# Transposing the second half of x with VectorE and transfers instead of TensorE

## The chip, the cores and the metric

The kernel runs on one core of a Trainium2 chip. The core has five engines with queues of their own: TensorE (matrix products into PSUM), VectorE, ScalarE, GpSimd (called POOL in the profile) and SyncE (SP, which here only issues transfers). The metric is the device time of one execution in microseconds. Times of runs are compared by their median; the profile covers one execution.

## What is computed

Two branches on the same x (2048 tokens, 448 features) are mixed by a gate for each token. Branch A is a diagonal state space layer with complex states, branch B a two-layer network with 1792 hidden units. All inputs are bf16.

```python
x = A_x                                   # [1, 2048, 448]
g = sigmoid((x * gate_w).sum(-1, keepdims=True))
# A: Lam_bar = exp(dt * Lam), B_bar = ((Lam_bar - 1) / Lam)[:, None] * Bmat
Bu = einsum("bld,pd->blp", x, B_bar)
for t in range(L):
    h = Lam_bar * h + Bu[:, t, :]
a = 2.0 * einsum("blp,dp->bld", hseq, Cmat).real + x * Dskip    # hseq: all h
b = silu(x @ w1) @ w2
return g * a + (1 - g) * b
```

## The kernel before

**Tiles and stages.** The tokens are cut into four stretches of 512 (`NCH = 4`, `CH = 512`), numbered 0 to 3. x is loaded with tokens on the partitions (`xnat`), four blocks of 128 tokens to a stretch. The products with w1 and with B contract over the features, so they need x with features on the partitions: `xT`. The 448 features are covered by four column groups of 128 that start at `XCOL = [0, 128, 256, 320]`; the last two overlap.

For each stretch: transposes of x (`x0_transposes` for stretch 0, `x_transposes` at line 498 for the others), products with w1 (tiles F) and B (tiles B) in `x_products` (matmul at line 663), evictions of the products from PSUM in `evict` (line 623): F tiles by ScalarE with silu into `aT` (line 634), B tiles into `U`, whose seven slots hold the states' inputs; for stretch 0 VectorE copies them (line 640), for the others ScalarE (line 642). Then `lanes` (line 706) on VectorE turns U by a rotation (COS, SIN), runs seven scans along the tokens (line 736) that write `Gf`, and turns the result back into `H`, one tensor for each stretch. For stretches 0 to 2 the scan's result comes back as bf16 (into U) by transfers that POOL issues (line 390). `ffn2` (line 768, matmul at 774) is the second layer of B, evicted by ScalarE (line 780) and added to the rest by an accumulating transfer of POOL (line 782). `readout` (line 786, matmul at 795) is the product of H with C, combined by VectorE (line 798) and stored by SP (line 801). `gates` (line 833) makes the gate and multiplies `xnat` in place by Dskip.

A transpose of stretches 1 to 3 is 32 TensorE transposes of 64 x 64 blocks into two PSUM banks (line 508), and two copies of 1024 elements into `xT`, by ScalarE (line 518) or, for one half of stretch 1, by VectorE (line 516).

**Order.** TensorE's order is the program's: the calls in the last lines of the kernel (864 to 883). All other engines are ordered by a list planner (`Plan.order`, line 104) when the kernel is built. It gives each operation a start by an estimated cost; among the operations of an engine that could start earliest it takes the one with the lowest priority number. In the calls `DVE(fn, reads, writes, cost, prio)` and `P.add(engine, ...)` the last numbers are these. `lanes(tc)` has priority 20 + tc, `gates` 19, parameters 3 to 3.5, U evictions 2.6 on VectorE and 5 on ScalarE. An issue of a load costs 0.5 us on SP, its data are put at 300 GB/s in one pipe, with 0.9 us ahead and 0.8 behind. On the chip each engine keeps the planned order and waits with semaphores (`Waits.put`) for what an operation reads or overwrites, however late that is.

Names that the change touches: `H[3]` is the state of stretch 3 and, early in the run, holds B's rows (`Bnat`) as they were loaded; after their transposes it lies unused until `lanes(3)`. `xn2`, `xn3` are the names of the loads of stretches 2 and 3; SP issues them last of all loads.

Of the kernel before, what the change touches and what calls it, by code (L numbers as in the profile page):

```python
# [11 lines left out]
BF16 = DT.bfloat16  # L12
I32 = DT.int32

S_TOK = 2048
D_MOD = 448
F_FF = 1792
CH = 512
# [4 lines left out]
NOT = 5  # L23
NWARM = 6
NFILL = 2
XCOL = [0, 128, 256, 320]

TURN = 6.283184
# [248 lines left out]
def bass_gated_mix__ssm_conv_s5__dense_activation_silu__prompt_kernel(nc, A_x, A_Lambda_re, A_Lambda_im, A_B_re, A_B_im, A_C_re, A_C_im,  # L277
               A_log_dt, A_Dskip, B_x, B_w1, B_w2, gate_w, out):
    with ExitStack() as ctx:
# [6 lines left out]
        x2, out2 = A_x[0], out[0]  # L286

        xnat = sb("xnat", [128, NTB, D_MOD], BF16)
        xT = sb("xT", [128, 4, S_TOK], BF16)
        w1s = sb("w1s", [128, 4, F_FF], BF16)  # L290
        w2s = sb("w2s", [128, NFB, D_MOD], BF16)
        BT = sb("BT", [128, 4, 896], BF16)
# [175 lines left out]
        def x0_transposes(q0, part, who):  # L468

            tk = Ps(2)  # L470

            def mm(pe):
                for q in (q0, q0 + 1):
                    for k in range(2):
                        o = ((q - q0) * 2 + k) * 64
                        for h in range(2):
                            p = slice(64 * h, 64 * h + 64)
                            r = pe.transpose(bk(tk, h).bitcast(BF16)[:, o:o + 64], xnat[p, 2 * part + k, XCOL[q]:XCOL[q] + 128], ident[p, p])  # L478
                return r
            PE(mm, [f"xn0{part}", "ident"], [tk], 4 * 0.054, "xT0")  # L480
            for h in range(2):
                src = lambda h=h: bk(tk, h).bitcast(BF16)[:, 0:256].rearrange("p (q b n) -> p q b n", q=2, n=64)
                dst = xT[:, q0:q0 + 2, 256 * part:256 * part + 256].rearrange("p q (b h n) -> p q b h n", h=2, n=64)[:, :, :, h, :]
                names = [f"xT0_{q}{part}{h}" for q in (q0, q0 + 1)]
                if who[h] == "d":
                    DVE(lambda e, src=src, dst=dst: e.tensor_copy(dst, src()), [tk], names, 0.28, 0, "xTe")  # L486
                else:
                    ACT(lambda e, src=src, dst=dst: e.activation(dst, src(), AF.Copy), [tk], names, act_cost(256), 0, "xTe")
# [4 lines left out]
        x0_transposes(2, 1, "dd")  # L493

        xn_of = {tc: {q: [f"xT{tc}_{h}" for h in range(2)] for q in range(4)} for tc in range(1, NCH)}
        xn_of[0] = {q: [f"xT0_{q}{part}{h}" for part in range(2) for h in range(2)] for q in range(4)}

        def x_transposes(tc, who):

            tk = Ps(2)  # L500

            def mm(pe):
                for q in range(4):
                    for b in range(4):
                        o = (q * 4 + b) * 64
                        for h in range(2):
                            p = slice(64 * h, 64 * h + 64)
                            r = pe.transpose(bk(tk, h).bitcast(BF16)[:, o:o + 64],  # L508
                                             xnat[p, 4 * tc + b, XCOL[q]:XCOL[q] + 128], ident[p, p])
                return r  # L510
            PE(mm, [f"xn{tc}", "ident"], [tk], 16 * 0.035, f"xT{tc}")
            for h in range(2):
                src = lambda h=h: bk(tk, h).bitcast(BF16).rearrange("p (q b n) -> p q b n", q=4, b=4)
                dst = xT[:, :, tc * CH:(tc + 1) * CH].rearrange("p q (b h n) -> p q b h n", h=2, n=64)[:, :, :, h, :]
                if who[h] == "d":
                    DVE(lambda e, src=src, dst=dst: e.tensor_copy(dst, src()), [tk], [f"xT{tc}_{h}"], 0.69, 2.2, "xTe")
                else:
                    ACT(lambda e, src=src, dst=dst: e.activation(dst, src(), AF.Copy), [tk], [f"xT{tc}_{h}"], act_cost(1024), 2.2, "xTe")

        cosn = [f"COS{k}" for k in range(4)] + ["COSd"]  # L520
        sinn = [f"SIN{k}" for k in range(4)] + ["SINd"]
# [101 lines left out]
        def evict(pair, tk):  # L623

            kinds = [t[0] for t in pair]
            for k, n in ((0, 2),) if pair[0][:2] == pair[-1][:2] and len(pair) == 2 else ((0, 1), (1, 1))[:len(pair)]:
                kind, tc, a = pair[k]
                step = pair[k + 1][2] - a if n == 2 else 1
                sl = slice(a, a + step * (n - 1) + 1, step)
                names = [t[2] for t in pair[k:k + n]]  # L630
                src = (lambda: bk2(tk)) if n == 2 else (lambda k=k: bk(tk, k)[:, None, :])
                if kind == "F":
                    dst = aT[tc % 2][:, sl, :]
                    ACT(lambda e, src=src, dst=dst: e.activation(dst, src(), AF.Silu),  # L634
                        [tk, "tbl"], [f"aT{tc % 2}_{m}" for m in names], act_cost(512 * n), 2.5, "silu")
                    continue
                U, un = UG[tc % 2], f"U{tc % 2}_"
                dst = U[:, sl, :]
                if tc == 0:
                    DVE(lambda e, src=src, dst=dst: e.tensor_copy(dst, src()), [tk], [f"{un}{m}" for m in names], 0.15 + 0.53 * n, 2.6, "U")  # L640
                else:
                    ACT(lambda e, src=src, dst=dst: e.activation(dst, src(), AF.Copy), [tk], [f"{un}{m}" for m in names], act_cost(512 * n), 5, "U")  # L642
                if 3 in names:
                    load("pool", U[0:64, 7, :], U[64:128, 3, :], un + "7a", 65536, 9, [un + "3"])
                    load("pool", U[64:128, 7, :], U[0:64, 3, :], un + "7b", 65536, 9, [un + "3"])

        def x_products(tiles, fill={}, wait=()):

            part = (list(zip([(i, 64) for i in (0, 1, 2, 3)], [(i, 0) for i in (0, 1, 3, 2)])),
                    list(zip([(i, 0) for i in (0, 1, 2)], [(i, 64) for i in (0, 1, 3)])))
            pairs = [tiles[t:t + 2] for t in range(0, len(tiles), 2)]
            toks = [Ps(2) for _ in pairs]

            def steps(k, h, a, z):
                def body(pe):
                    for n, cut in list(enumerate(part[h]))[a:z]:  # L660
                        for b, ((i, p0), tile) in enumerate(zip(cut, pairs[k])):
                            tc = tile[1]
                            r = pe.matmul(bk(toks[k], b), weights(tile, p0, p0 + 64, i), xT[p0:p0 + 64, i, tc * CH:(tc + 1) * CH],  # L663
                                          start=(h == 0 and n == 0), stop=(h == 1 and n == 2))
                    return r
                reads = [n for cut in part[h][a:z] for (i, _), tile in zip(cut, pairs[k])
                         for n in xn_of[tile[1]][i] + (w1n(tile[2], i) if tile[0] == "F" else btn[tile[2]])]
                return PE(body, list(dict.fromkeys(reads)), [toks[k]], (z - a) * PE_MM[512], f"{pairs[k][0][0]}{pairs[k][0][1]}")

            def half(k, h):  # L670
                if h == 0 and pairs[k][0] == ("F", 0, 0):
                    def zero(pe):
                        for n in range(NFILL):
                            for b, p in enumerate((slice(64, 128), slice(0, 64))):
                                r = pe.matmul(bk(toks[k], b)[:, 0:128], ones[p, 0:128], ones[p, 0:128], start=True, stop=True)  # L675
                        return r
                    PE(zero, [], [toks[k]], NFILL * 0.11, "fill")
                    steps(k, 0, 0, 2)
                    steps(k, 0, 2, 4)
                else:  # L680
                    steps(k, h, 0, len(part[h])).own = h == 1
                if h:
                    evict(pairs[k], toks[k])

            half(0, 0)
            for f in fill.get(-1, ()):
                f()
            for k in range(len(pairs)):
                order = [lambda: half(k, 1)] + [lambda: half(k + 1, 0)] * (k + 1 < len(pairs))
                for n, f in enumerate(order if k - 1 in wait else order[::-1]):  # L690
                    f()
                    for m in fill.get((k, n), ()):
                        m()
                for f in fill.get(k, ()):
                    f()
# [173 lines left out]
        gates(0)  # L869
        gates(1)  # L870
        lanes(1)
        for f in cp(0) + G(0, 1) + cp(1, 2) + G(2, 3) + cp(3):
            f()
        x_products(F(1) + F(2, 0, 1) + B(2), {2: xt(2, "aa")})
        gates(2)
        lanes(2)
        for f in G(4, 5, 6, 7) + C(0, 1, 2, 3):
            f()
        x_products(F(2, 1) + B(3) + F(3), {1: xt(3, "aa"), 9: [lambda: gates(3), lambda: lanes(3)]})
        for f in C(4, 5, 6, 7) + G(8, 9, 10, 11):  # L880
            f()
        for f in C(8, 9, 10, 11) + G(12, 13, 14, 15) + C(12, 13, 14, 15):
# [36 lines left out]
```

## Time and profile before

| what | us |
|---|---|
| runs: median of three (lowest, highest) | 141.94 (141.46, 142.53) |
| the profiled execution | 141.25 |
| its span | 139.5 |
| TensorE busy | 135.9 |
| VectorE busy | 122.0 |
| ScalarE busy | 90.3 |
| POOL busy | 39.2 |
| L663, products with xT, share of the chain | 46% |
| L774, second layer of B, share of the chain | 31% |
| L795, readout, share of the chain | 15% |
| L508, transposes of stretches 1 to 3, share of the chain | 1% |
| SP, last issue of a load; first store | 21.8; 70.3 |

The span runs from the first to the last instruction in the profile; 1.75 us of the execution lie around it. All times inside the profile count from the span's start. Engine names with q (SPq) are the queue's own work: issues of transfers. The chain of work that ended last is followed back from the last instruction to whatever released it. "Idle before" an instruction is in brackets with what ended it. In the profile UG is the tensor that holds U.

### The profile page before, as it was taken

The numbers are of one execution on the slowest core, as the hardware profiler recorded it, in microseconds if no ns is written. First come the engines' busy times: TensorE is split into PE (matmuls) and PEld (weight loads), VectorE is DVE, ScalarE is ACT, GpSimd is POOL, SyncE is SP. The second block draws the span as 40 slices with busy tenths as digits, with TensorE's granted clock in tenths as the row PEclk, the third lists the DMA queues.
The fourth block names the chain that finished last, engine by engine and source line by source line (L and its number), as shares of the span: only waits on it lengthen the run. The fifth ranks groups of instructions, "written<-read, shape, count | busy, mean of one in ns | idle before, by whom it ended". The sixth has DMA issues, their size and how long they took to land.

```text
span 139.5 us, 3000 instructions
## 1 busy us (share of the span) xinstructions
PE 135.9 (97%) x1201; PEld 67.0 (48%) x1201; DVE 122.0 (87%) x179; ACT 90.3 (65%) x157; POOL 39.2 (28%) x72
## 2 busy tenths in 40 slices
PE   7999999999999999999999999999999999999992
PEld 2445454455544544455544544444455555555561
DVE  0319999999999999999999999999999999997053
ACT  3349768999989999823694887799931268312300
POOL 7134040100248440227733001824000314022220
PEclk9999999999999999999999999999999999999999
DMA  4998999510156770104976200674202322323242
GB/s 136 337 294 243 363 320 238 177 42 0 31 79 94 129 110 1 38 15 73 157 131 155 38 5 0 95 133 79 38 4 97 66 33 36 83 83 61 40 94 71
DMA packets 17956, 14.71 MB, mean 105 GB/s; under 512 B 2835, under 2 KB 17814, under 8 KB 17942
## 3 DMA queue, kind: packets, MB, share of 16 engines
q0 software_dynamic: 6064, 5.51, 24.8%
q1 hardware_dynamic: 11318, 8.65, 20.7%
q10 hardware_dynamic: 560, 0.36, 0.8%
q8 instruction: 9, 0.15, 0.4%
q14 instruction: 5, 0.04, 0.1%
HBM read 7.17 MB, written 1.84 MB: 65 GB/s over the span
## 4 chain that ended last, share of the span: by engine, by line
PE 97%; DVE 0%; issue 0%
PE ps L663 46%; PE ps L774 31%; PE ps L795 15%; PE ps L463 2%; PE ps L508 1%; PE ps L478 1%; PE ps L814 1%; PE ps L604 1%; DVE ot L798 0%; PE ps L675 0%; PE ps L464 0%; PE ps L536 0%
## 5 line engine op out<-in xcount | busy, mean ns | idle before, releaser
L663 PE MATMUL ps<-xT,w1s 64*128 64x512 bf16 x392 | 48.5, 378 | 0.0
L774 PE MATMUL ps<-w2s,aT 128*128 128x448 bf16 x224 | 43.2, 353 | 0.0
L634 ACT ACTIVATE aT<-ps 128x1024 bf16<-128x1024 f32 (+1 forms) x30 | 28.7, 969 | 8.5 <-PE ps L663 8.4
L774 PEld LDWEIGHTS ps<-w2s,aT 128*128 128x128 bf16 x224 | 21.7, 98 | 20.4 <-ACT xnat L849 0.4
L663 PEld LDWEIGHTS ps<-xT,w1s 64*128 64x128 bf16 x392 | 19.7, 94 | 22.3 <-DVE xT L486 0.7
L663 PE MATMUL ps<-xT,BT 64*128 64x512 bf16 x196 | 25.8, 376 | 0.0
L782 POOL DMA_DIRECT2D xnat<-fe x16 | 14.1, 900 | 37.9 <-ACT fe L780 37.2
L780 ACT ACTIVATE fe<-ps,g 128x448 bf16<-128x448 f32 x16 | 10.1, 632 | 21.1 <-PE ps L774 21.0
L390 POOL DMA_DIRECT2D UG<-Gf x27 | 14.7, 549 | 20.9 <-DVE Gf L736 20.4
L736 DVE TENSOR_TENSOR_SCAN Gf<-rc,gin,H 128x512 f32<-128x512 f32 x14 | 17.2, 1268 | 0.0
L795 PE MATMUL ps<-CP,H 128*128 128x448 bf16 (+2 forms) x98 | 16.4, 326 | 0.0
L663 PEld LDWEIGHTS ps<-xT,BT 64*128 64x128 bf16 x196 | 10.8, 94 | 11.1 <-DVE Gf L562 0.2
L798 DVE SCALAR_TENSOR_TENSOR ot<-ps,g,xnat 128x448 bf16<-128x448 f32 (+2 forms) x18 | 10.8, 622 | 6.0 <-issue 4.6
L390 POOL DMA_DIRECT2D UG<-UG x8 | 4.8, 597 | 29.2 <-ACT UG L642 17.4
L704 DVE TENSOR_TENSOR H<-UG,COS 128x3584 bf16<-128x3584 bf16 (+4 forms) x10 | 12.6, 1266 | 0.0
L795 PEld LDWEIGHTS ps<-CP,H 128*128 128x128 bf16 x98 | 8.9, 98 | 7.5 <-DVE k L752 0.4
L642 ACT ACTIVATE UG<-ps 128x1024 bf16<-128x1024 f32 (+1 forms) x12 | 10.7, 923 | 1.4 <-PE ps L663 1.4
L842 ACT ACTIVATE junk<-xg 128x448 bf16<-128x448 bf16 x16 | 9.2, 574 | 2.1 <-DVE xg L704 2.0
L849 ACT ACTIVATE xnat<-xnat,g 128x448 bf16<-128x448 bf16 x16 | 9.8, 671 | 0.2
L704 DVE TENSOR_TENSOR PI<-UG,SIN 128x512 bf16<-128x512 bf16 (+2 forms) x13 | 9.1, 722 | 0.0
L704 DVE TENSOR_TENSOR PO<-UG,SIN 128x1536 bf16<-128x1536 bf16 (+1 forms) x8 | 8.7, 1087 | 0.1
L736 DVE TENSOR_TENSOR_SCAN Gf<-rc,gin,H2C 128x512 f32<-128x512 f32 x7 | 8.5, 1265 | 0.0
(102 smaller groups left out, 126.5 us busy)
## 6 DMA issues: line engine op xcount, KB each, us to landing
UG<-Gf POOLq DMA_DIRECT2D x21, 128.0 KB, 2.5
xnat<-fe POOLq DMA_DIRECT2D x16, 112.0 KB, 2.6
out_dram<-ot SPq DMA_DIRECT2D x15, 112.0 KB, 1.7
w2s<-in_B_w_dram SPq DMA_DIRECT2D x1, 1568.0 KB, 11.8
xnat<-in_A_x_dram SPq DMA_DIRECT2D x3, 448.0 KB, 6.1
w1s<-in_B_w_dram SPq DMA_DIRECT2D x1, 576.0 KB, 6.2
UG<-UG POOLq DMA_DIRECT2D x8, 64.0 KB, 2.2
H2C<-in_A_C_re_dram SPq DMA_DIRECT2D x2, 196.0 KB
```

Of the source, the lines that this page charges most:

```text
L390: P.add(q, lambda e: e.dma_start(dst, src), list(after), name.split(), 0.6 if q == "pool" else 0.5, prio, sem(), nbytes, tag="ld " + name)
L634: ACT(lambda e, src=src, dst=dst: e.activation(dst, src(), AF.Silu), [tk, "tbl"], [f"aT{tc % 2}_{m}" for m in names], act_cost(512 * n), 2 ...
L642: ACT(lambda e, src=src, dst=dst: e.activation(dst, src(), AF.Copy), [tk], [f"{un}{m}" for m in names], act_cost(512 * n), 5, "U")
L663: r = pe.matmul(bk(toks[k], b), weights(tile, p0, p0 + 64, i), xT[p0:p0 + 64, i, tc * CH:(tc + 1) * CH], start=(h == 0 and n == 0), stop=( ...
L704: DVE(lambda e: e.tensor_tensor(o, a, b, op), r, w, dve_cost(n, 2), prio, tag)
L736: DVE(lambda e, s=s, b=b, init=init: e.tensor_tensor_scan(Gf[:, s, :], rc[:, b:b + 1].to_broadcast([128, CH]), A[:, s, :], init, ALU.mult, ...
L774: r = pe.matmul(bk(tk)[:, 0:D_MOD], aT[tc % 2][:, fb, o:o + 128], w2s[:, fb, :], start=(fb == 0), stop=(fb == NFB - 1))
L780: ACT(lambda e: e.activation(f[:, :], bk(tk)[:, 0:D_MOD], AF.Copy, scale=g1[:, tb:tb + 1]), [tk, f"g1_{tc}"], [fn], act_cost(448, 1), 7, "fe")
L782: P.add("pool", lambda e: e.dma_start(Tb[:, tb, :], f[:, :], accum_op=ALU.add), [fn, f"Tb{tb}"], [f"Tb{tb}"], 0.94, 2, sem(), 115000, tag= ...
L795: r = pe.matmul(bk(tk)[:, 0:b - a], H[tc][:, s, o:o + 128], CP[:, s, a:b], start=(s == 0), stop=(s == NSLOT - 1))
L798: DVE(lambda e, tk=tk, a=a, b=b: e.scalar_tensor_tensor(ot[tb % NOT][:, a:b], bk(tk)[:, 0:b - a], g[:, tb:tb + 1], Tb[:, tb, a:b], ALU.mul ...
L849: ACT(lambda e, tb=tb: e.activation(Tb[:, tb, :], xnat[:, tb, :], AF.Copy, scale=g[:, tb:tb + 1]), [f"xd{tc}", f"g_{tc}"], [f"Tb{tb}"], ac ...
```

## The change

x of stretches 2 and 3 is no longer transposed by TensorE. `x_blocks(tc)` has VectorE transpose `xnat` in blocks of 32 by 32 into a scratch that lies in `H[3]`, with four instructions (two token blocks at a time, first the three column groups from 0, then the one from 320). In such a transpose each group of 32 partitions stays in place, so what is still to be done is to carry blocks from one partition group to another: 16 transfers (4 source groups g, 4 target groups m), each from 32 partitions to 32 partitions, 512 runs of 64 bytes, 32 KB, issued by SP with priority 400. Both stretches use the same scratch, so the transposes of stretch 3 wait for the transfers of stretch 2. The transposes have priority 15 for stretch 2 and 20.5 for stretch 3.

`xT` is laid out with the stretch first and the column group second. Of the seven U slots of stretch 0, evicted as (0, 1), (2, 3), (4, 5) and (6), the last three go to ScalarE.

```diff
+XPRIO = {2: 15, 3: 20.5}
+XBLK = (2, 3)
+UDVE = (0, 2)
...
-        xT = sb("xT", [128, 4, S_TOK], BF16)
+        xT = sb("xT", [128, NCH, 4, CH], BF16)
...
+        for tc in XBLK:
+            xn_of[tc] = {q: [f"xT{tc}_{g}{m}" for g in range(4) for m in range(4)] for q in range(4)}
...
+        def x_blocks(tc):
+
+
+            X32 = H[3][:, 0:4, :].rearrange("p m (q b i) -> p m q b i", q=4, i=32)
+            names = [f"H3_{s}" for s in range(7)] + ["H3_3i"]
+            xs = xnat[:, 4 * tc:4 * tc + 4, :]
+            for q0, q1, c in ((0, 3, 0), (3, 4, XCOL[3])):
+                n = q1 - q0
+                for b0, b1 in ((0, 2), (2, 4)):
+                    src = xs[:, b0:b1, c:c + 128 * n].rearrange("p b (q m i) -> p b q m i", q=n, i=32)
+                    dst = X32.rearrange("p m q b i -> p b q m i")[:, b0:b1, q0:q1, :, :]
+                    DVE(lambda e, dst=dst, src=src: e.transpose(dst, src), [f"xn{tc}"], names, 0.15 + 256 * n / 960, XPRIO[tc], "xTd")
+            k = sem()
+            for g in range(4):
+                for m in range(4):
+                    to = xT[32 * m:32 * m + 32, tc, :, :].rearrange("p q (b g i) -> p (q b) g i", b=4, i=32)[:, :, g, :]
+                    P.add("sp", lambda e, to=to, g=g, m=m: e.dma_start(to, X32[32 * g:32 * g + 32, m, :, :, :].rearrange("p q b i -> p (q b) i")),
+                          names, [f"xT{tc}_{g}{m}"], 0.5, 400, k, 32768, tag="xTm")
...
-                if tc == 0:
+                if tc == 0 and a in UDVE:
                     DVE(lambda e, src=src, dst=dst: e.tensor_copy(dst, src()), [tk], [f"{un}{m}" for m in names], 0.15 + 0.53 * n, 2.6, "U")
                 else:
                     ACT(lambda e, src=src, dst=dst: e.activation(dst, src(), AF.Copy), [tk], [f"{un}{m}" for m in names], act_cost(512 * n), 5, "U")
...
-                            r = pe.matmul(bk(toks[k], b), weights(tile, p0, p0 + 64, i), xT[p0:p0 + 64, i, tc * CH:(tc + 1) * CH],
+                            r = pe.matmul(bk(toks[k], b), weights(tile, p0, p0 + 64, i), xT[p0:p0 + 64, tc, i, :],
...
         lanes(1)
+        if 2 in XBLK:
+            x_blocks(2)
         for f in cp(0) + G(0, 1) + cp(1, 2) + G(2, 3) + cp(3):
             f()
-        x_products(F(1) + F(2, 0, 1) + B(2), {2: xt(2, "aa")})
+        if 3 in XBLK:
+            x_blocks(3)
+        x_products(F(1) + F(2, 0, 1) + B(2), {2: xt(2, "aa")} if 2 not in XBLK else {})
...
-        x_products(F(2, 1) + B(3) + F(3), {1: xt(3, "aa"), 9: [lambda: gates(3), lambda: lanes(3)]})
+        x_products(F(2, 1) + B(3) + F(3), {1: xt(3, "aa") if 3 not in XBLK else [], 9: [lambda: gates(3), lambda: lanes(3)]})
```

More of the change, by code (lines that the diff above doesn't have):

```diff
@@ L482, in x0_transposes @@
                 src = lambda h=h: bk(tk, h).bitcast(BF16)[:, 0:256].rearrange("p (q b n) -> p q b n", q=2, n=64)
-                dst = xT[:, q0:q0 + 2, 256 * part:256 * part + 256].rearrange("p q (b h n) -> p q b h n", h=2, n=64)[:, :, :, h, :]
+                dst = xT[:, 0, q0:q0 + 2, 256 * part:256 * part + 256].rearrange("p q (b h n) -> p q b h n", h=2, n=64)[:, :, :, h, :]
                 names = [f"xT0_{q}{part}{h}" for q in (q0, q0 + 1)]
@@ L513, in x_transposes @@
                 src = lambda h=h: bk(tk, h).bitcast(BF16).rearrange("p (q b n) -> p q b n", q=4, b=4)
-                dst = xT[:, :, tc * CH:(tc + 1) * CH].rearrange("p q (b h n) -> p q b h n", h=2, n=64)[:, :, :, h, :]
+                dst = xT[:, tc, :, :].rearrange("p q (b h n) -> p q b h n", h=2, n=64)[:, :, :, h, :]
                 if who[h] == "d":
```

## The prediction

> **What bounds the kernel now.** I began with the page's busy shares and the chain that ended last, in order of time. Columns of the chain: start, length, what ran.
>
> ```profile
> PE 135.9 (97%) x1201; PEld 67.0 (48%) x1201; DVE 122.0 (87%) x179; ACT 90.3 (65%) x157; POOL 39.2 (28%) x72
> ```
>
> ```profile
> 45.55 0.47 PE ps L508 x32
> ...
> 77.23 0.47 PE ps L508 x32
> ...
> 131.38 5.35 PE ps L795 x42
> 136.73 0.02 issue
> 136.75 0.35 DVE ot L798
> ```
>
> TensorE is the chain from 0.76 to 136.73 us with no gap. The two L508 entries, the TensorE transposes of x's third and fourth stretch, are what the change takes out of it.
>
> Then the timeline of VectorE, because the change adds work there:
>
> ```profile
> 18.43 1.22 DVE L640 CAST UG<-ps 128x1024 bf16<-128x1024 f32 x1
> 19.57 0.42 DVE L524 TENSOR_SCALAR Gf<-Gf 128x512 f32<-128x512 f32 x1
> 19.90 0.68 DVE L640 CAST UG<-ps 128x512 bf16<-128x512 f32 x1
> 20.50 0.68 DVE L516 COPY xT<-ps 128x1024 bf16<-128x1024 bf16 x1
> ...
> 42.73 5.67 DVE L736 TENSOR_TENSOR_SCAN Gf<-rc,H 128x512 f32<-128x512 f32 x5
> 48.32 2.00 DVE L704 TENSOR_TENSOR H<-UG,COS 128x3584 bf16<-128x3584 bf16 x1
> ...
> 126.07 2.09 DVE L704 TENSOR_TENSOR H<-H,PO 128x2048 bf16<-128x2048 bf16 x2
> 132.80 0.69 DVE L798 SCALAR_TENSOR_TENSOR ot<-ps,g,xnat 128x448 bf16<-128x448 f32 x1 [4.64 <-issue]
> ```
>
> VectorE has practically no idle time from 14 us until 128.16 (126.07 + 2.09), when it finishes H3, the state of the last stretch. TensorE reads H3 first at 131.38. So VectorE has a slack of 3.22 us, about 3.1 after the 0.1 that the planner counts for the signal, and everything added to its queue after 14 us, work or waiting, comes off this slack one for one. TensorE is the bound with a second bound 3 us behind it.
>
> Last the DMA view, cut to two windows: 15.9 to 18.6 us (rows of 896 B) and 22.0 to 22.5 (mostly the 128 B rows of C).
>
> ```profile
> DMA packets 1153, 1.03 MB, mean 381 GB/s; under 512 B 6, under 2 KB 1153, under 8 KB 1153
> q1 hardware_dynamic: 1153, 1.03, 109.0%
> ```
>
> ```profile
> DMA packets 228, 0.09 MB, mean 186 GB/s; under 512 B 151, under 2 KB 224, under 8 KB 228
> q1 hardware_dynamic: 216, 0.08, 84.5%
> ```
>
> Shares are of 16 engines. An 896 B packet held an engine 1.09 x 16 x 2.7 / 1153 = 40.8 ns. In the second window 0.845 x 16 x 0.5 = 6.76 us; less 65 large ones (2.65) leaves 151 small ones 27 ns each. The same sum gives 13 ns in 21.6 to 22.0 and 48 ns in 22.5 to 23.0. A small packet is not much cheaper than a large one.
>
> **The change part by part.** *TensorE* loses 2 x 0.47 = 0.94 us. That is all the change can gain: everything else in the chain stays. The new layout of xT costs nothing: the moving operand is 512 contiguous elements before and after (L663, 376 to 378 ns); nothing covers it, so a slower read would go straight into the span.
>
> *ScalarE* takes over one eviction of two slots and one of a single slot: 1.03 + 0.60 us by its own L642 rows, about 1.4 as starts follow ends 0.1 early. It loses four L518 copies, 1.95 at 46.51 and 1.93 at 78.19. Its idle pieces between 16 and 22 us (0.91, 0.84, 0.40, 0.47) hide the addition. Without that cover the banks of U come free up to 1.4 us late and TensorE waits for a bank; 0.94 of it would be paid by the transposes that fall away.
>
> *VectorE* loses the 18.43 and 19.90 casts: start to start 1.14 + 0.60 = 1.74 us. It gains eight transposes, per stretch two of 768 elements per partition and two of 256, together 2048. No row shows a transpose. Bounds: the quickest form, the SBUF copy of 1536 bf16 in 0.53, is 0.25 ns an element with the 0.146 fixed that L704 shows (3584 in 2.006, 512 in 0.412); the slowest, the scan, 512 in 1.26, is 2.15 ns. In the middle stands L798: 448 in 0.673, 128 in 0.346, so 1.02 ns. Their geometric middle is 0.73, and L798 is the nearest row; I take it. With 0.07 net per instruction: 2048 x 1.02 ns + 0.28 = 2.37 us a stretch, 4.7 for both; bounds 1.6 and 9.4.
>
> The first set waits for the load xn2, issued at 21.30 and 5.5 us in flight, so there at 26.8. The planner has it sooner: 6.87 MB of loads up to it at its 300 GB/s is 22.9, with 0.72 + 0.9 + 0.8 around it 25.3. VectorE runs in planned order, so it can stand still up to 1.5 us; behind it stand the rest of the parameters, lanes(0) (first at 27.51) and all that follows. I take 0.7. Dependent instructions and returns of Gb that share the DMA engines cost a little: 0 to 2, taken 0.3 (64 KB copies of POOL took 6.4 to 6.5 us beside the loads at 16 to 21 us, 2.2 in the median, but the last returns of stretch 0, issued after 48.7, come when the new transfers are nearly through).
>
> Sum for VectorE: + 4.7 - 1.74 + 0.7 + 0.3 = + 4.0. H3 is ready at 132.1 and TensorE, which comes to it at 130.4, starts at about 132.2, against 131.38: + 0.9 us. The tail behind it is unchanged. In the profiled execution (span 139.5, 141.25 in all, 1.75 around it) that gives 140.4 and 142.15; the median of the three runs is 141.94, 0.69 above the profiled one, so I set **142.8**.
>
> *The transfers* are the second question. Each set is 16 issues on SP of 512 runs of 64 B, 32 per engine, 512 per engine for a set. SP is idle from 23 to 70 us, so nothing is queued behind the first set. The second goes out from about 55 us, and if the queue backs up as it did for 5.37 us at 10.62, the stores from 70.3 on wait behind it. They release five output buffers of which four are filled by 75, the sixth readout is at 103: 28 us of cover. First set: transposes, interleaved with other ready work, end near 30.5; 1.6 us for issue to landing as the stores show; 512 x 27 ns = 13.8; so 45.9. POOL's own transfers of 36.7 to 46, eight of them at some 0.55 us of every engine (43% of 36.7 to 40 for two and a half), may add up to 4.5: 50.4.
>
> Who waits: TensorE needs xT of stretch 2 for the pair (F2, B2), 92 matmuls of 0.108 after 40.15, at 50.1. And VectorE: the second set of transposes writes the same scratch, so it waits until all 16 transfers have read it. The planner counts 0.5 an issue and 0.11 of data, so it thinks the scratch free near 40. Priority 20.5 keeps the transposes behind the lanes(0) work at 20, to the end of the scans, where priority 21 work now starts at 48.32; moved by what is then added (2.4 - 1.74 + 0.7), 49.6. So both readers come at 49.6 to 50.1 for data that is there at 45.9 to 50.4: between 3.7 us of cover and 0.8 late. I take it as just in time. The second set needs 55 + 1.6 + 13.8, some 3 more for POOL, 73.5; its reader stands 78 matmuls after 72.8, at 81.2.
>
> The Trainium skill (DMA: Bandwidth & Descriptors, Why small descriptors are slow) says that transfers inside SBUF are spared the small-descriptor penalty; no row of this trace tests it. By that rule both sets are early and the sum above stands unchanged, with the next rival gone.
>
> **Rivals.** *Late transfers (slower).* At 33 ns a packet, still inside 13 to 48, and with POOL's share, the first set is there at 30.5 + 1.6 + 16.9 + 4.5 = 53.5. VectorE stands still 3.9 us in front of the second set, with lanes(1) behind it, and H3 moves by as much: + 4.8, 146.7. It decides from 25 ns with POOL's whole share, from 34 without. At 48 ns it would be + 12.5. For it: 48 and 39 ns in two of the windows. Against: those reads come from HBM and in a mix with large ones; these stay in SBUF. The Trainium skill (DMA: Bandwidth & Descriptors, Specifications) gives 512 B as the least size for full rate, with read-modify-write below; that speaks for this rival.
>
> *The full gain.* If a transpose runs at a bf16 tensor_tensor's 0.52 ns, both sets take 2.7 us and VectorE's sum is + 1.0 to + 2.0, within 3.1. Then TensorE stays the bound: - 0.94, 141.0. For it: operand and result are bf16 in SBUF, as in L704. Against: the result goes back in another order than it came.
>
> *Slow transposes.* At the scan's rate, 9.4: VectorE + 8.7, + 5.6 at the end, 147.5. Only the scan, a recurrence, is so slow.
>
> *It does not do what it says*: the two L508 groups would still stand in the profile. The edited lines leave no call for stretches 2 and 3; under 1 in 100.
>
> **How the numbers follow.** My case, VectorE late by about 1 us with the transfers in time, 0.46 (its own range, with 0 to 2.5 us for the two waits together, is 141.8 to 144.3); late transfers 0.32; the full gain 0.15; slow transposes 0.06; else 0.01. About 1% is what a measurement of this kernel can tell from no change: 140.5 to 143.4. Faster by more than that is beyond the 0.94 there is, so only scatter gives it: 0.04. Within: 0.38 of my case, 0.11 of the gain, 0.05 of transfers late by under a microsecond: 0.54. Slower: 0.42. The range goes from 140.9 (the full gain, a little scatter) to 148.0, which leaves out the late transfers above 36 ns and the worst of slow transposes, about 2 in 10 with the lower edge.
>
> **What would show it.** Right: no L508 after 20 us; eight transposes of some 0.95 and 0.4 us; the chain leaving TensorE for VectorE's H3 before the last readouts; a short wait of VectorE for the load near 26 us; H3 done near 132. Wrong: TensorE unbroken to the end (gain), a wait of VectorE or of L663 for a transfer near 50 us (late transfers), transposes of 0.5 or 1.8 us. I would be most wrong if 64 B packets inside SBUF cost 40 ns or more, or if the planner puts the second set earlier than the end of the scans.

## The result and the profile after

| | median us (lowest to highest) | ratio to the kernel before, 95% interval |
|---|---|---|
| before, same chip | 141.72 (141.45 to 142.53) | |
| changed | 143.63 (143.11 to 144.83) | 1.014 (1.010 to 1.018) |

Some executions of a kernel run in a slower state, and the medians and ratios given here and below leave them out. The changed kernel is 1.4% slower. Its profiled execution took 143.16 us with a span of 141.4, 1.9 more than before. New lines in the file shift the numbers: the products are L687, the second layer L798, the readout L819 with its combination L822, the second layer's eviction into the two buffers fe L804 and the accumulating transfer from there L806, the transposes left on TensorE L513, U's evictions L664 (VectorE) and L666 (ScalarE), VectorE's products L728; the new transposes are L536, the new transfers L541.

Busy shares on the page of the changed kernel, then its chain (start, length, what):

```profile
PE 135.2 (96%) x1137; PEld 65.7 (46%) x1137; DVE 125.0 (88%) x185; ACT 88.4 (63%) x155; POOL 38.7 (27%) x72
```

```profile
132.66 0.05 issue
132.71 5.52 PE ps L819 x42
138.23 0.03 issue
138.26 0.35 DVE ot L822
```

The chain no longer goes back through TensorE to the start: it begins at 132.66, where TensorE takes up the last readouts. What it waited for is in the timeline of TensorE (in brackets the idle time before and what ended it) and in that of VectorE:

```profile
3.90 0.90 PE L481 MATMUL ps<-ident,xnat 64*128 64x64 bf16 x32 [0.20 <-DMA xnat<-in_A_x_dram]
6.16 3.02 PE L687 MATMUL ps<-xT,w1s 64*128 64x512 bf16 x26 [0.46 <-DMA w1s<-in_B_w_dram]
22.22 0.37 PE L687 MATMUL ps<-xT,w1s 64*128 64x512 bf16 x1 [0.25 <-DVE nn L593]
43.71 7.94 PE L687 MATMUL ps<-xT,w1s 64*128 64x512 bf16 x71 [0.38 <-ACT fe L804]
132.71 5.50 PE L819 MATMUL ps<-CP,H 128*128 128x448 bf16 x42 [0.91 <-DVE H L728]
```

```profile
25.98 0.16 DVE L593 TENSOR_TENSOR scc<-asum,inv 128x8 f32<-128x8 f32 x1
27.16 0.98 DVE L536 STREAM_TRANSPOSE H<-xnat 128x768 bf16<-128x768 bf16 x1 [1.01 <-DMA xnat<-in_A_x_dram]
...
30.57 0.43 DVE L536 STREAM_TRANSPOSE H<-xnat 128x256 bf16<-128x256 bf16 x1
...
50.41 0.96 DVE L536 STREAM_TRANSPOSE H<-xnat 128x768 bf16<-128x768 bf16 x1
51.29 0.13 DVE L776 TENSOR_TENSOR k<-Gf,CC 128x7 f32<-128x7 f32 x1
...
130.56 2.09 DVE L728 TENSOR_TENSOR H<-H,PO 128x2048 bf16<-128x2048 bf16 x2
134.30 0.69 DVE L822 SCALAR_TENSOR_TENSOR ot<-ps,g,xnat 128x448 bf16<-128x448 f32 x1 [1.65 <-issue]
```

Two things are to be seen. VectorE finishes H3 at 132.65 and TensorE starts at 132.71, so VectorE's work sets the end, with a wait of 1.01 us for a load in it. And TensorE, which had no gap before, has small ones at 4, 6, 22 and 43 us; it came to the last readouts at 131.80 (132.71 - 0.91), not at the 130.4 that two transposes less would give. The gaps at 4 and 6 us are waits for loads, earlier than anything that the change touches.

The new transfers disturb nobody by being late. DMA queues of the changed kernel from 33 to 36 us, when only they run (packets; share of 16 engines):

```profile
DMA packets 2421, 0.15 MB, mean 50 GB/s; under 512 B 2421, under 2 KB 2421, under 8 KB 2421
q1 hardware_dynamic: 2421, 0.15, 43.6%
```

0.436 x 16 x 3 / 2421 is 8.6 ns for a packet. The 16 issues of stretch 2 run from 31.0 to 42.2 us, 0.7 each, and this spacing, not the packets, sets their pace: with an eighth of the data (`e9_late_eighth`, below) the 16 issues still take 10.8 us, 0.60 each in the median. From 44 to 48 us only 62 packets are left on this queue, so the set is through near 44 us, 6 us ahead of both readers; the transposes at 50.41 follow without a wait.

### The profile page after: what moved, and what is told of

It is laid out like the page before. It is cut to its first block, busy times and chain, and to the rows that moved or that the text cites. A ratio compares the mean times of both kernels' runs of the same rounds, so it can differ in the third digit from the quotient of the medians.

```text
span 141.4 us, 2908 instructions
## 1 busy us (share of the span) xinstructions
PE 135.2 (96%) x1137; PEld 65.7 (46%) x1137; DVE 125.0 (88%) x185; ACT 88.4 (63%) x155; POOL 38.7 (27%) x72
## 5 line engine op out<-in xcount | busy, mean ns | idle before, releaser
L687 PE MATMUL ps<-xT,w1s 64*128 64x512 bf16 x392 | 48.2, 376 | 1.1 <-DMA w1s<-in_B_w_dram 0.5
L798 PE MATMUL ps<-w2s,aT 128*128 128x448 bf16 x224 | 43.2, 353 | 0.0
L798 PEld LDWEIGHTS ps<-w2s,aT 128*128 128x128 bf16 x224 | 21.7, 98 | 20.4 <-issue 0.4
L687 PEld LDWEIGHTS ps<-xT,w1s 64*128 64x128 bf16 x392 | 19.7, 94 | 24.0 <-DVE xT L489 0.9
L687 PE MATMUL ps<-xT,BT 64*128 64x512 bf16 x196 | 25.8, 376 | 0.0
L806 POOL DMA_DIRECT2D xnat<-fe x16 | 14.0, 895 | 41.7 <-ACT fe L804 34.2
L804 ACT ACTIVATE fe<-ps,g 128x448 bf16<-128x448 f32 x16 | 10.1, 634 | 20.6 <-PE ps L798 19.6
L393 POOL DMA_DIRECT2D UG<-Gf x27 | 14.4, 541 | 20.9 <-DVE Gf L760 20.5
L819 PE MATMUL ps<-CP,H 128*128 128x448 bf16 (+2 forms) x98 | 16.4, 326 | 0.9 <-DVE H L728 0.9
L687 PEld LDWEIGHTS ps<-xT,BT 64*128 64x128 bf16 x196 | 10.7, 94 | 11.1 <-ACT aT L658 0.5
L666 ACT ACTIVATE UG<-ps 128x1024 bf16<-128x1024 f32 (+1 forms) x14 | 12.2, 919 | 3.3 <-DVE H L728 1.4
L822 DVE SCALAR_TENSOR_TENSOR ot<-ps,g,xnat 128x448 bf16<-128x448 f32 (+2 forms) x18 | 10.9, 624 | 3.0 <-issue 1.6
L819 PEld LDWEIGHTS ps<-CP,H 128*128 128x128 bf16 x98 | 8.8, 98 | 8.6 <-DVE H L728 1.4
L728 DVE TENSOR_TENSOR H<-UG,COS 128x3584 bf16<-128x3584 bf16 (+4 forms) x10 | 12.6, 1264 | 0.0
L728 DVE TENSOR_TENSOR PI<-UG,SIN 128x512 bf16<-128x512 bf16 (+2 forms) x13 | 9.1, 721 | 0.0
L728 DVE TENSOR_TENSOR PO<-UG,SIN 128x1536 bf16<-128x1536 bf16 (+1 forms) x8 | 8.5, 1084 | 0.0
```

Of the source, the lines that this page charges most:

```text
L393: P.add(q, lambda e: e.dma_start(dst, src), list(after), name.split(), 0.6 if q == "pool" else 0.5, prio, sem(), nbytes, tag="ld " + name)
L728: DVE(lambda e: e.tensor_tensor(o, a, b, op), r, w, dve_cost(n, 2), prio, tag)
L798: r = pe.matmul(bk(tk)[:, 0:D_MOD], aT[tc % 2][:, fb, o:o + 128], w2s[:, fb, :], start=(fb == 0), stop=(fb == NFB - 1))
L804: ACT(lambda e: e.activation(f[:, :], bk(tk)[:, 0:D_MOD], AF.Copy, scale=g1[:, tb:tb + 1]), [tk, f"g1_{tc}"], [fn], act_cost(448, 1), 7, "fe")
L806: P.add("pool", lambda e: e.dma_start(Tb[:, tb, :], f[:, :], accum_op=ALU.add), [fn, f"Tb{tb}"], [f"Tb{tb}"], 0.94, 2, sem(), 115000, tag= ...
L819: r = pe.matmul(bk(tk)[:, 0:b - a], H[tc][:, s, o:o + 128], CP[:, s, a:b], start=(s == 0), stop=(s == NSLOT - 1))
```

## The experiments

The theory to be tested: VectorE's net work and its wait for the load set the end. Two rivals: ScalarE's three U slots cost TensorE time, and the new transfers slow others. In the diffs only the changed lines stand. All ratios are to the kernel before, on the same chip; its median there lies between 141.47 and 141.72 us, so small differences between kernels are read from the ratios.

**The U evictions alone** (`e1_uact_only`).

```diff
-XBLK = (2, 3)
+XBLK = ()
```

> Only the U evictions of the change: stretches 2 and 3 are transposed by TensorE again, three U slots of stretch 0 stay with ScalarE (xT in the new layout). Theory (VectorE is the bound of the changed kernel): VectorE loses 1.74 us and has some 5 us of slack, TensorE is the bound as before, 141.7 or up to 0.3 more. Rival (ScalarE's extra work makes TensorE wait): TensorE shows the two waits of the changed kernel, 0.25 near 22 us and 0.38 near 43 us, in this one too, and the time is 0.6 above the kernel before, 142.3.

Measured: 142.14 us, ratio 1.0027 (1.0004 to 1.0051). H3 is done at 127.21, 5 us ahead of its reader, so VectorE is not the bound. TensorE waits 0.25 us at 22 us but has no wait near 43. The time lies between the two expectations. ScalarE's evictions, with the new layout of xT, cost a quarter of a per cent; not all of it is ScalarE's, as TensorE was already 0.6 us late at 9.4 us after a wait for a load of w1. The wait near 43 us needs something else than the evictions.

**The blocks alone** (`e2_blocks_only`).

```diff
-UDVE = (0, 2)
+UDVE = (0, 2, 4, 6)
```

> Only the transposes by VectorE and the transfers: all seven U slots of stretch 0 stay with VectorE. Theory: VectorE has 1.74 us more work than in the changed kernel, of which at most the 1.0 us wait for the load is hidden; H3 is done 0.7 to 1.7 us later, the time is 144.3 to 145.4. Rival (ScalarE): the TensorE waits near 22 and 43 us are gone and the time falls to about 143.0.

Measured: 144.34 us, ratio 1.020 (1.0168 to 1.0231), 0.7 above the changed kernel. VectorE has 1.74 us more to do, its wait for the load shrinks from 1.01 to 0.53, and H3 is done at 133.61, 0.96 later than in the changed kernel. The time moved about as H3 moved, as the theory has it. The wait of 0.25 at 22 us is gone. The one near 43 us is there, and larger (0.75, for fe), with no U slot of stretch 0 on ScalarE: it is not those evictions that make it. With VectorE last it doesn't count, nor does one of 0.3 for a U eviction at 88 us.

**Stretch 3 alone** (`e3_stretch3_only`).

```diff
-XBLK = (2, 3)
+XBLK = (3,)
```

> Only stretch 3 in blocks; TensorE transposes stretch 2 (0.47 us more on TensorE), three U slots with ScalarE. Theory: VectorE loses 2.5 us of transposes and the wait of 1.0 us, H3 is done near 129.2 and TensorE is the bound again: 0.47 less than the kernel before plus whatever TensorE waits for ScalarE; 141.3 without such waits. Rival (ScalarE): the waits of 0.6 us stay, 141.9 or more.

Measured: 141.34 us, ratio 0.9979 (0.9958 to 0.9999). H3 is done at 129.56 and TensorE is the bound again; its wait at 22 us (0.25) is there, that near 43 isn't. A tie with the kernel before, or a trace faster. Without stretch 2 in blocks the loss of the changed kernel is gone.

**The wait for the load taken away** (`e4_planned_late`).

```diff
-                 x2[tc * CH:(tc + 1) * CH, :].rearrange("(b p) d -> p b d", p=128), f"xn{tc}", CH * 896)
+                 x2[tc * CH:(tc + 1) * CH, :].rearrange("(b p) d -> p b d", p=128), f"xn{tc}", CH * 896 + (600000 if tc == 2 else 0))
```

> The changed kernel with the planner told that the load of stretch 2 takes 2 us longer, so that VectorE does five operations of stretch 0 ahead of the first transpose; the order of all other engines is the same. Theory: the wait of 1.0 us for the load is gone or nearly so, H3 is done near 131.7, TensorE comes to it at 131.8 and both are bounds: 0.9 less than the changed kernel, 142.7. Rival (VectorE is not what sets the end): no change, 143.6.

Measured: 144.35 us, ratio 1.0213 (1.016 to 1.0267; three of four executions lie from 144.07 to 144.36, the fourth at 146.02): both theories missed. The wait for the load is gone, but the kernel is no faster than the changed one, and rather slower: the span of its profiled execution is 142.5 us against 141.4, though the intervals of the ratios just overlap. Waits of this kernel, by total, times and longest:

```profile
PE ps L687 <- ACT fe L804: 2.0, 1, 2.0
...
PE ps L819 <- DVE H L728: 0.5, 1, 0.5
```

and the row of ScalarE that TensorE waited for:

```profile
44.57 0.63 ACT L804 ACTIVATE fe<-ps,g 128x448 bf16<-128x448 f32 x1 [2.35 <-DMA xnat<-fe]
```

The wait of 0.38 us near 43 has become 2.0. TensorE needs a PSUM bank that ScalarE is to empty into one of two fe buffers, and ScalarE waits 2.35 us until POOL's accumulating transfer has read the buffer. VectorE, running ahead, then stands 1.59 us at 71.81 for a readout that TensorE delivers late, so H3 comes at 133.78 after all. A second cost shows: in the window of the new transfers (31 to 44 us) the accumulating transfers took longer. Issues of this kernel there, with the median time to landing last:

```profile
xT<-H SPq DMA_DIRECT2D x15, 32.0 KB, 2.5
xnat<-fe POOLq DMA_DIRECT2D x3, 112.0 KB, 4.2
```

In the kernel before they took 2.8 us in that window:

```profile
xnat<-fe POOLq DMA_DIRECT2D x4, 112.0 KB, 2.8
```

**Stretch 2 alone** (`e5_stretch2_only`): `XBLK = (2,)`.

> Only stretch 2 in blocks; TensorE transposes stretch 3; three U slots with ScalarE. H3 is done near 130.2, so VectorE isn't the bound. Theory now (a second cost: the transfers of stretch 2 share the DMA engines with the accumulating transfers of POOL, which free the two fe buffers, so that ScalarE's eviction and behind it TensorE wait near 43 us): TensorE keeps a wait of 0.3 to 2 us there, 142.2 to 144. Rival (the transfers disturb nobody, VectorE's sum alone counts): no such wait, 141.4 as with stretch 3 only.

Measured: 143.29 us, ratio 1.0131 (1.0081 to 1.018), as slow as the whole change. H3 is done at 132.52, TensorE comes at 133.17: here TensorE is the bound. Its timeline:

```profile
43.48 7.94 PE L687 MATMUL ps<-xT,w1s 64*128 64x512 bf16 x71 [0.69 <-ACT fe L804]
96.09 5.36 PE L687 MATMUL ps<-xT,w1s 64*128 64x512 bf16 x48 [1.12 <-ACT aT L658]
```

The wait near 43 us is there without stretch 3, and a later one follows from VectorE's lateness: ScalarE stands 2.95 us for VectorE's `xg` (for the gate) at 94.46 with the eviction that TensorE needs queued behind it. VectorE itself had stood 1.61 us for the load and 1.57 for the return of a scan's result at 80.78. The expected mechanism is there, the larger wait of the two I had not foreseen.

**Four fe buffers** (`e6_four_fe`), which takes ScalarE's reason to wait away.

```diff
-        fe = [sb(f"fe{k}", [128, D_MOD], BF16) for k in range(2)]
+        fe = [sb(f"fe{k}", [128, D_MOD], BF16) for k in range(4)]
...
-            f = fe[tb % 2]
-            fn = f"fe{tb % 2}"
+            f = fe[tb % 4]
+            fn = f"fe{tb % 4}"
```

> The changed kernel with four fe buffers instead of two, so that ScalarE need not wait for an accumulating transfer before it evicts; the order of TensorE, VectorE, POOL and SP is the same. Theory: TensorE's wait of 0.38 near 43 us is gone, but H3 still comes at 132.6 from VectorE, so the time stays at 143.6. Rival (TensorE's waits set the end): 143.2 or less.

Measured: 143.13 us, ratio 1.010 (1.0072 to 1.0127). The wait near 43 is gone, H3 comes at 132.47, and TensorE waits for it 1.1 us instead of 0.9. By the number the rival has it, as 143.13 is below its 143.2, but the intervals of this and of the changed kernel (1.010 to 1.018) overlap, so the time doesn't show that anything was gained. The trace tells the two apart: VectorE is still the last, and TensorE starts at 132.53, right behind H3.

**Late plan and four buffers** (`e7_late_four_fe`): the edits of the last and of `e4_planned_late` together.

> Both: the planner told that the load of stretch 2 comes later, and four fe buffers. Theory: without the later load's wait (1.0 us) on VectorE and without the wait of 2.0 us that TensorE had near 43 us in the kernel with the late plan alone, H3 is done near 131.7 and TensorE comes at 131.4: 142.6, that is 1.0 below the changed kernel and 2.5 below the late plan with two buffers. Rival (something else made that kernel slow): 144 or more.

Measured: 142.07 us, ratio 1.0043 (1.0021 to 1.0064), 1.06 below four buffers alone, which ran beside it, and well below the late plan alone (1.0213 there). Neither remedy does much by itself. TensorE's last wait, and VectorE's end:

```profile
131.17 5.50 PE L819 MATMUL ps<-CP,H 128*128 128x448 bf16 x42 [0.47 <-DVE H L728]
```

```profile
129.03 2.09 DVE L728 TENSOR_TENSOR H<-H,PO 128x2048 bf16<-128x2048 bf16 x2
```

H3 at 131.12, TensorE at 130.70: VectorE is still the bound, by half a microsecond, and 2.96 us later than before the change.

**Stretch 3 alone, all U slots on VectorE** (`e8_stretch3_u_dve`): `XBLK = (3,)`, `UDVE = (0, 2, 4, 6)`.

> Only stretch 3 in blocks, and all seven U slots of stretch 0 with VectorE as before the change: VectorE has 2.5 us more than before, H3 near 130.7 to 131.3; TensorE is rid of 0.47 us and comes at 130.9. Theory: both bounds nearly meet, 141.3 to 141.6, no more than 0.3 from the kernel with three slots on ScalarE. Rival (ScalarE's three slots cost TensorE time): 0.3 or more faster than that one, 141.1.

Measured: 140.87 us, ratio 0.9959 (0.9931 to 0.9987), below the range of the theory. It beats the kernel before, by 0.4%. In its timelines H3 is done at 130.76 and TensorE starts the last readouts at 130.82 with no wait of its own for ScalarE:

```profile
130.82 5.50 PE L819 MATMUL ps<-CP,H 128*128 128x448 bf16 x42
```

```profile
128.67 2.09 DVE L728 TENSOR_TENSOR H<-H,PO 128x2048 bf16<-128x2048 bf16 x2
```

The kernel with three slots on ScalarE (`e3_stretch3_only`) stood at 0.9979, 0.2% higher; that speaks for the rival, that those slots cost TensorE time, but the intervals overlap (0.9958 to 0.9999 there), so the size isn't settled.

**An eighth of the data in the transfers** (`e9_late_eighth`), for the second cost.

```diff
+XH = {2: slice(0, 2), 3: slice(0, 16)}
...
-                    to = xT[32 * m:32 * m + 32, tc, :, :].rearrange("p q (b g i) -> p (q b) g i", b=4, i=32)[:, :, g, :]
+                    to = xT[32 * m:32 * m + 32, tc, :, :].rearrange("p q (b g i) -> p (q b) g i", b=4, i=32)[:, XH[tc], g, :]
...
+        POOL(lambda e: e.memset(xT[:, 2, :, :], 0.0), [], [f"xT2_{g}{m}" for g in range(4) for m in range(4)], 1.2, 3)
```

The source is cut with the same slice.

> The kernel with the late plan and two fe buffers, with an eighth of the data in the 16 transfers of stretch 2 (2 of the 16 runs of 64 B in each partition); the other seven eighths of that stretch's xT are zeros that POOL writes at the start, so stretch 2 is computed from wrong numbers. The order of all engines is the same but for that one POOL instruction. Theory (the transfers of stretch 2 slow the accumulating transfers on the shared DMA engines): those land in about 2.8 us again instead of 4.2 in 31 to 44 us, TensorE's wait of 2.0 us near 43 us falls to 0.5 or less, 142.6 to 143.4. Rival (it was the order of ScalarE alone): the wait stays at about 2 us, 145.

Measured: 142.68 us, ratio 1.0088 (1.0058 to 1.0118), against 1.0213 for the same order with all the data. Of TensorE's wait near 43 us only 0.1 is left (it is busy 19.89 of the 20 us from 40 on), ScalarE's before the fe row is 0.52, and the accumulating transfers from 31 to 44 us land in 2.8 us:

```profile
xnat<-fe POOLq DMA_DIRECT2D x4, 112.0 KB, 2.8
xT<-H SPq DMA_DIRECT2D x16, 4.0 KB, 2.0
```

The number of issues and the order of all compute engines are those of `e4_planned_late`, but for one POOL instruction near the start. The eviction into fe for which TensorE waited starts at 43.05 instead of 44.57, which is 1.5 of the 1.9 us that the wait lost; TensorE's own lateness hides the rest, as it came to this place 0.3 us later, after a wait of 0.75 for w1 near 6 us. So it is the data of the new transfers that holds up the accumulating ones. That isn't all that makes fe late, though. In the changed kernel the second fe buffer is full at 37.83, but its transfer is issued only at 39.89: POOL waits until ScalarE has scaled the rows of xnat that it adds to, which in the new order stands behind the third eviction. In the kernel before ScalarE scales these rows ahead of that eviction, and the transfer goes out near 38.9.

**Two more U slots on ScalarE** (`e10_late_four_fe_u2`): `UDVE = (0,)` on top of `e7_late_four_fe`.

> The kernel with the late plan and four fe buffers, with two more U slots of stretch 0 (five of seven) on ScalarE: VectorE loses another 1.14 us, H3 near 130.0. Theory: TensorE becomes the bound; without waits for ScalarE it comes to H3 at 130.5, 141.3 or a little less. Rival (ScalarE is full between 15 and 45 us and TensorE waits longer for it than VectorE gains): 142.1 or more.

Measured: 143.03 us, ratio 1.0116 (1.0097 to 1.0135). H3 is ready at 130.95, only 0.17 earlier than in `e7_late_four_fe` instead of the 1.1 expected (0.49 of it is a wait of VectorE for a return at 79.85; the rest wasn't traced). But TensorE comes at 132.56, after waits at 22 and 24 us:

```profile
21.68 1.69 PE L687 MATMUL ps<-xT,w1s 64*128 64x512 bf16 x14 [1.38 <-DVE prq L593]
23.72 0.39 PE L687 MATMUL ps<-xT,w1s 64*128 64x512 bf16 x1 [0.35 <-ACT UG L666]
```

The rival was right here. The releaser named in the first line is a small VectorE operation that TensorE doesn't need. The wait ends 0.14 us behind ScalarE's copy of its half of stretch 1's xT (20.52 + 1.02), and so it does in the changed kernel (the copy ends at 22.08, the wait at 22.22), in the kernel with the late plan and four buffers (21.54, 21.68) and in that with the U evictions alone (22.36, 22.50). Whether TensorE waits for that half of xT or for the two banks that the copy empties isn't told apart. The two kernels with all U slots on VectorE have the copy at 20.2 and no such wait. The copy in the kernel before and in the changed one:

```profile
20.17 1.02 ACT L518 ACTIVATE xT<-ps 128x1024 bf16<-128x1024 bf16 x1
```

```profile
21.06 1.02 ACT L523 ACTIVATE xT<-ps 128x1024 bf16<-128x1024 bf16 x1
```

## Why the prediction was right, step by step

The forecast, 142.8 us with VectorE late by about 1 us and the transfers in time, had the mechanism. Measured were 143.63, inside the range but above 143.4, up to which I had counted the time as no change: the slower side, to which I had given 0.42 against 0.54 for within. In the profiled execution the forecast was 142.15 and 143.16 was measured. Of the difference of 1.0, 0.5 is VectorE's sum (H3 at 132.65 instead of 132.1) and 0.4 lies behind the last readouts, in the tail that I had called unchanged.

- *VectorE's transposes*: right. Start to start they take 2.50 and 2.49 us a stretch against 2.37 forecast; 768 and 256 elements in 0.98 and 0.43 are 1.07 ns an element (1.02 taken). That a transpose runs at nearly the rate of L798, a different instruction, had no reason but that L798 was the nearest row, so the good size has luck in it.
- *Its wait for the load*: 1.01 us against 0.7, between the bounds 0 and 1.5. By the sum, 4.99 - 1.74 + 1.01 = 4.26, and the measured delay of H3 is 4.49 (132.65 against 128.16). The remainder of 0.23 is in the 0.3 set for small things, but it isn't what the 0.3 was set for: VectorE was already 0.36 late at 15 us, before anything of the change.
- *Place of the second set*: forecast at 49.6, measured at 50.41, right behind the scans.
- *TensorE's gain of 0.94 and ScalarE's cover*: this step failed. I had ScalarE's idle pieces hide the evictions of its three slots, but the first of them, at 18.53, and the order that goes with it push its copy of stretch 1's xT from 20.17 to 21.06 (0.36 of that lateness was there before them), which makes TensorE stand 0.25 us. Behind that, an eviction into fe that came late makes it stand 0.38; this one comes with stretch 2's blocks and not with the evictions of U, since `e2_blocks_only` and `e5_stretch2_only` have it and `e1_uact_only` and `e3_stretch3_only` don't. TensorE came to the last readouts at 131.80, 0.4 later than before (131.38) instead of 0.9 earlier. Set beside the timeline before, it is 0.36 late at 19.8 us by the loads, 0.80 late at 28.9 behind the wait at 22, gains 0.94 by the transposes and loses 0.55 near 43. In the changed kernel VectorE covers this loss; without stretch 3's transposes on VectorE TensorE is the bound itself (`e5_stretch2_only`). So of the two bounds that I saw, both moved later.
- *The transfers in time*: right, by 6 us, for another reason than I reckoned, and so by luck. A packet of 64 B took 8.6 ns, not 27, and the pace was the issue's 0.7 us. The Trainium skill's statement (DMA: Bandwidth & Descriptors, Why small descriptors are slow) that transfers inside SBUF are spared the small-descriptor penalty agrees with this trace in part: 8.6 ns is less than the 13 to 48 of the small reads from HBM, but 64 B in 8.6 ns is 7.4 bytes a nanosecond, a third of the 22 of the 896 B packets (40.8 ns). The rival of late transfers was priced from the wrong rows.
- *What the transfers do to others*: I had set POOL's share on their finish, not theirs on POOL's. The accumulating transfers lengthened (2.8 to 4.2 us in the late plan, 2.9 in the changed kernel) and two fe buffers let that through to TensorE. `e9_late_eighth` shows the cause for the late plan, `e6_four_fe` and `e7_late_four_fe` the cover. In the changed kernel they lengthened little, and the late issue of one of them (39.89) is as likely a cause of its 0.38; no run separates the two there.
- *The full gain* fell with the transposes' real rate; *slow transposes* too.

Of the 1.9 us between the two profiled spans, 1.5 lie ahead of the last readouts (TensorE starts them at 132.71 against 131.22 in the timeline) and 0.4 behind VectorE's last instruction. The prediction had that tail unchanged, and this step failed. The piece behind VectorE's last instruction is 2.3 to 2.4 us in the kernel before and in the four with one stretch in blocks or none, and 2.7 to 2.9 in all seven with both. So it goes with the change: one of SP's last store issues (the one at 138.04 in the changed kernel) comes 0.89 us ahead of the next in six of the seven and 0.77 in `e9_late_eighth`, where the other five kernels have 0.38 to 0.50, and SP issues them one after the other. Why that issue is slow stayed open. Open too is the wait of 0.3 to 0.8 us for the first w1 load near 6 us, which eight of the eleven kernels profiled after the change show, and three of them and the kernel before don't; nothing ahead of it differs in order on TensorE, and it wasn't tried.

## What to carry to other kernels

Where a second engine is full and is done 3 us before the first needs its result, work moved to it is paid from those 3 us: the last stretch alone (2.5 us) fitted and paid, both didn't. Nor did the earlier stretch alone, which brought a wait for its load and traffic beside other transfers. When work goes to an engine's idle pieces, look at what is queued behind it there, and not only at the sum: one more eviction gave TensorE a wait of 0.25 us by way of a copy that came late. And where a new stream of transfers shares time with transfers that free a buffer, count the buffers: with two, a wait of 1.0 us that was removed on VectorE came back as 2.0 on TensorE.

## What the runs showed of the hardware that was not expected

A VectorE transpose of bf16 in 32 by 32 blocks runs at 1.07 ns an element, as L798 before (f32 from PSUM, 1.02), and not at the 0.52 of a bf16 product. Packets of 64 B inside SBUF held an engine for 8.6 ns, a third of the 27 that I had counted with, while each transfer of 32 KB in the changed kernel held SP's queue 0.59 to 0.91 us (median 0.63), so that 16 of them need 11 us; with an eighth of the data it held the queue 0.60 and the 16 needed 10.8. Beside the new transfers, an accumulating transfer of 112 KB took 4.2 us in the median in the late plan, where they had 32% of the DMA engines' time from 31 to 44 us, and 2.9 in the changed kernel, where they had 38%, against 2.8 before: half again as long or hardly longer, and the share doesn't tell which.
